# Block 0 of a one-core attention and two-expert-layer kernel: later weight splits, squares on GpSimd, single loads, two raw pieces on SP's queue

## The chip, the cores and the metric

The kernel runs on one core of one Trainium2 chip. The metric is the device time of one execution in microseconds; three executions of the kernel before are shown. One execution was also profiled, and every row below is from that one.

## What is computed

Attention with four sink tokens and a window of 128 feeds a dense layer with a squared relu, and its output feeds a layer of eight experts, of which each token uses one. The reference, cut to what matters:

```python
# q, k, v: (4, 8, 768, 64); x: 3072 tokens x 512
scores = q @ k.T / sqrt(64);  keep = is_sink | in_window        # 4 sinks, window 128
a = softmax(where(keep, scores, -1e9));  x = a @ v              # -> (3072, 512)
h = maximum(x @ w_in, 0);  x = (h * h) @ w_out                  # w_in 512 x 2048, w_out 2048 x 512
e = argmax(x @ w_gate);  g = softmax(x @ w_gate)[e];  o = sigmoid(x @ w_output_gate)[e]
out = g * o * (maximum(x @ w1[e], 0) @ w2[e])                   # 8 experts, 512 x 1024 x 512
```

The inputs `w_in` and `w_out` arrive as 64-bit floats and are turned into 32-bit ones on the chip.

## The kernel before

The 3072 tokens are 12 blocks of 256. For each block t the program makes attention (four pairs p of heads, two row groups n) and then the dense layer in 16 slices j: `l1(t, j)` multiplies by 128 columns of `w_in` and squares the relu, `l2(t, j)` multiplies by the matching rows of `w_out` and adds up in PSUM, two slices behind. The attention of block t + 1 is laid between the slices of block t. The expert layer follows after block 11, in an order written out by hand.

The order of all else is found by a planner: instructions are handed to it in the order of the program, some with a raised priority, and it fills each engine's queue by estimated times. `tc.keep_in_program_order` (also `pin`) holds instructions of one engine in the order of the program, and `behind(x, y)` places x after y without a semaphore of its own.

Weights of the dense layer come in 32 raw pieces of 512 KB (`conv(c)`; c = 2j is slice j of `w_in`, c = 2j + 1 slice j of `w_out`). The raw form has two 32-bit words for each number. Pieces 0 to 2 (`NBOOT`) have buffers of their own, `braw`, and are issued from ScalarE's queue; the others go from SP's queue into the tag "stage" with three buffers, which a few other tiles share. The inner `rest()` makes the 32-bit weights: two ScalarE activations (L327, L330) and two VectorE merges (L334, L335) into `fw[n]`, or into `fbuf` for the last eight slices of `w_out`. Block 0 multiplies by `fw` as they are ("native", L677 and L706). All other multiplications use a split into a high and a low part: `fin()` makes the high part on ScalarE (L338) and the low part on VectorE (L339). For `fbuf` it runs at once. For the native weights the program keeps it in `fins` and calls it 12 (`w_in`) or 13 (`w_out`) slices after the weights' own (`LAGS`); its subtraction waits for the native matmul that reads the weights, its ScalarE copy for nothing but the weights.

`cstep(1)` runs the next `rest()` and `fetch` issues the DMA of the next pieces but one. Ahead of block 0 a loop over half-slices h from -46 to -1 calls it at every third h, beside the attention of block 0. In block 0 it is called with each slice.

`loads(t, p, kinds)` fetches q, k and v of one pair of heads; `more(t, p)` calls it for the pair two further on. Some loads of block 0 are also called explicitly ahead of that: for pair 2, k and q are loaded by the explicit call and again by `more(0, 0)`, into the next of two buffers, and the dictionary `nat` holds the later one. `fill` issues dummy matmuls in block 0.

Of the kernel before, what the change touches and what calls it, by code (L numbers as in the profile page):

```python
# [12 lines left out]
U32 = mybir.dt.uint32  # L13
AF = mybir.ActivationFunctionType
# [26 lines left out]
NBOOT = 3  # L41
# [6 lines left out]
def kern(ctx, tc, q, k, v, n_sink, window, w_in, w_out, w_gate, w_og, w1, w2, out):  # L48
    nc = tc.nc
    V, A, G, PE, SY = nc.vector, nc.scalar, nc.gpsimd, nc.tensor, nc.sync  # L50
# [9 lines left out]
    fw = [nc.alloc_sbuf_tensor_at(f"fw{n}", [128, 512], F32, offset=w0 + 4 * (1024 * n + 512)).ap() for n in range(NF + NF // 2)]  # L60
# [226 lines left out]

    fbuf = att.tile([128, 2, 512], F32, tag="PT", name="fbuf", bufs=1)

    fins, used = {}, {}  # L290

    def after(x, y):

# [5 lines left out]
    def behind(x, y=None):  # L299

        tc.add_manual_dep(x.ins, (y or skd[0]).ins.name, mybir.DependencyInfo(mybir.DependencyClass.NoSync, mybir.DependencyReason.DATA),
                          reason="order")
        return x

    def conv(c):
        j, which = divmod(c, 2)
        if c < NBOOT:
            raw, dq = braw[c], A
        else:
            raw = cv.tile([128, 512, 2], I32, tag="stage", bufs=3, name="craw")  # L310
            dq = SY
        if which == 0:
            x = dq.dma_start(out=raw[:].rearrange("p (k f) w -> p k (f w)", k=4),
                         in_=w_in.bitcast(I32)[:, 256 * j:256 * j + 256].rearrange("(k p) f -> p k f", p=128))
            hi, lo = (WI[:, j, n].rearrange("p k f -> p (k f)") for n in range(2))
        else:
            x = dq.dma_start(out=raw[:].rearrange("p f w -> p (f w)"), in_=w_out.bitcast(I32)[128 * j:128 * j + 128, :])
            hi, lo = (WO[j // 8][:, j % 8, n] for n in range(2))
        if c < NBOOT + 2:
            tc.keep_in_program_order(x)  # L320
        if c < NBOOT:
            behind(x, brd[0])

        def rest():
            L, Hh = raw[:, :, 0], raw[:, :, 1]

            x = A.activation(out=Hh.bitcast(F32), in_=Hh.bitcast(F32), func=AF.Copy, scale=2.0 ** -112)  # L327
            if c < NBOOT:
                tc.keep_in_program_order(x)
            A.activation(out=L, in_=L.bitcast(U32), func=AF.Copy, scale=0.93 * 2.0 ** -29)  # L330
            n = NF * which + j
            f = fw[n] if n < len(fw) else fbuf[:, j % 2]
            fi = f.bitcast(I32)
            V.scalar_tensor_tensor(out=fi, in0=Hh, scalar=3, in1=L, op0=ALU.logical_shift_left, op1=ALU.bitwise_or)  # L334
            V.scalar_tensor_tensor(out=fi, in0=Hh, scalar=-2147483648, in1=fi, op0=ALU.bitwise_and, op1=ALU.bitwise_or)  # L335

            def fin():
                A.activation(out=hi, in_=f, func=AF.Copy)  # L338
                x = V.tensor_tensor(out=lo, in0=f, in1=hi.bitcast(F32), op=ALU.subtract)  # L339
                if n < len(fw):  # L340
                    after(x, used[n])

            if n < len(fw):
                fins[n] = fin
            else:
                fin()
        return rest
# [9 lines left out]
    moe.tile([128, HOME // 4], F32, name="gap1", bufs=1)  # L357
    xTs = {}

    def loads(t, p, kinds="kqvs"):  # L360
        b, u = divmod(t, NQ // 2)
        s0 = 256 * u
        for nm, src, m in (("k", k, 3), ("q", q, 2), ("v", v, 3)):
            if nm not in kinds:
                continue
            x = att.tile([128, m, 2, D], F32, tag=nm + "n", name=nm + "n", bufs=3 if nm == "v" else 2)
            lo = s0 - 128 * (m - 2)
            o = 0
            if lo < 0:
                lo, o = 0, 1  # L370
            nb = m - o
            for e in range(2):
                x_ = (A if t == 0 and (nm == "q" and p < 2 or nm == "v" and p == 0) else SY).dma_start(out=x[:, o:m, e, :],
                             in_=src[b, 2 * p + e, lo:lo + 128 * nb, :].rearrange("(n s) d -> s n d", s=128))
                if t == 0 and (p >= 2 or nm == "v"):
                    pin(x_)
                if brd and t == 0 and p < 3:
                    behind(x_, brd[0])
            nat[nm, t, p] = x
        if u == 0 and p == 0 and "s" in kinds:  # L380
            x = att.tile([H * NS, D], F32, tag="vs", name="vs", bufs=1)
            x_ = SY.dma_start(out=x[:], in_=v[b, :, 0:NS, :])
            if t == 0:
                pin(x_)
            nat["vs", b] = x
# [115 lines left out]
    def scores(t, p, n):  # L501
        i = 2 * (t % 3) + n
        W = 128 if i == 0 else 260
        c0 = KS * n if i else KS
        mask = (M0, M1, M2)[min(i, 2)]
        qt = qTt[t, p]
        kt = kTt[t, p]
        if t == 0 and n % 2:
            ps = [psX.tile([128, 512], F32, tag=f"x{e}", name=f"psx{e}") for e in range(2)]
        else:  # L510
            ps = [psS.tile([128, 512], F32, tag=f"s{e}", name=f"pss{e}") for e in range(2)]
        if t == 0:
            fill(ps[0][:, 0:W], 2)
        for e in range(2 if t < T32 else 0):
            r = slice(64 * e, 64 * e + 64)
            PE.matmul(ps[e][:, 0:W], lhsT=qt[r, 0, n, :], rhs=kt[r, 0, c0:c0 + W].bitcast(F32), start=True, stop=True)
        for e in range(2 if t >= STK else 0):
            for a_ in range(2):
                PE.matmul(ps[e][:, 0:W], lhsT=qt[:, a_, e, n, :], rhs=kt[:, e, c0:c0 + W], start=(a_ == 0), stop=(a_ == 1))
        for m, (a_, b_) in enumerate(((0, 0), (0, 1), (1, 0)) if T32 <= t < STK else ()):  # L520
            for e in range(2):
                r = slice(64 * e, 64 * e + 64)
                PE.matmul(ps[e][:, 0:W], lhsT=qt[r, a_, n, :], rhs=kt[r, b_, c0:c0 + W], start=(m == 0), stop=(m == 2))
        P = att.tile([128, 2, 260], F32, tag="P", name="P", bufs=2)
        st = att.tile([128, 8], F32, tag="st", name="st", bufs=4)
        with (tc.high_priority(100) if t >= STK else ExitStack()):
            for e in range(2):
                V.tensor_tensor_reduce(out=P[:, e, 0:W], in0=ps[e][:, 0:W], in1=mask[:, 0:W], scale=-SCALE, scalar=3.0e38,  # L528
                                       op0=ALU.add, op1=ALU.min, accum_out=st[:, e:e + 1])
        for e in range(2):  # L530
            A.activation(out=P[:, e, 0:W], in_=P[:, e, 0:W], func=AF.Exp, scale=-1.0, bias=st[:, e:e + 1],  # L531
                         accum_out=st[:, 4 + e:5 + e])
        V.tensor_scalar(out=st[:, 6:8], in0=st[:, 4:6], scalar1=1e-9, scalar2=None, op0=ALU.add)
        V.reciprocal(out=st[:, 6:8], in_=st[:, 6:8])  # L534
        if t >= T32 and i >= 2:

            V.tensor_tensor(out=P[:, :, 0:128], in0=P[:, :, 0:128], in1=P[:, :, 132:260], op=ALU.add)
            W = KS
        for e in range(2):
            if t < T32 and t + e:  # L540
                V.tensor_scalar(out=P[:, e, 0:W], in0=P[:, e, 0:W], scalar1=st[:, 6 + e:7 + e], scalar2=None, op0=ALU.mult)
            else:
                A.activation(out=P[:, e, 0:W], in_=P[:, e, 0:W], func=AF.Copy, scale=st[:, 6 + e:7 + e])  # L543
        if i >= 2:
            o = psk[n][:, 2 * p:2 * p + 2, :]
            G.tensor_copy(out=o[:, :, 0:4], in_=P[:, :, 128:132])
            G.tensor_copy(out=o[:, :, 8:12], in_=P[:, :, 128:132])
            G.tensor_tensor(out=o[:, :, 4:8], in0=P[:, :, 128:132], in1=o[:, :, 0:4].bitcast(F32), op=ALU.subtract)
        Ptile[t, p, n] = P
# [122 lines left out]
    def l1(t, j):  # L672
        ps = psH.tile([128, 256], F32, tag="h", name="psh")
        x = xTs.get(0)
# [9 lines left out]
            for n, (kk, a_, b_) in enumerate(terms):  # L684
                PE.matmul(ps[:], lhsT=WI[:, j, a_, kk, :], rhs=x[:, b_, kk, :], start=(n == 0), stop=(n == 11))  # L685
        hq = moe.tile([128, 256], F32, tag="r", name="r", bufs=2)
        A.activation(out=hq[:], in_=ps[:], func=AF.Relu)  # L687
        E_ = G if t == 0 and j % 2 else V
        if t == 0 and NF + j < len(fw):
            o = moe.tile([128, 256], F32, tag="h2", name="h32", bufs=3, padded_shape=[128, 512])  # L690
            E_.tensor_tensor(out=o[:], in0=hq[:], in1=hq[:], op=ALU.mult)
# [220 lines left out]
    braw = [boot.tile([128, 512, 2], I32, name=f"braw{n}") for n in range(NBOOT)]  # L912
# [28 lines left out]
    for h in range(-46, 0):  # L941
        run_to(h)
        if h == -42:
            masks(wide, 1)
        if h == -24:
            setup2()
        if h >= -39 and h % 3 == 0:
            cstep(1)
    bootS.close()
    wpool2 = ctx.enter_context(tc.tile_pool(name="wpool2", bufs=1))  # L950
# [4 lines left out]
    raw = None  # L955
# [113 lines left out]
    for g in range(G2):  # L1069
        t, j = divmod(g, NF)  # L1070
# [42 lines left out]
    t = NBLK - 1  # L1113
# [151 lines left out]
```

## Time and profile before

| | us |
|---|---|
| median of three executions | 1129.04 (1128.1 to 1131.95) |
| the profiled execution, its own time | 1127.99 |
| its span, first to last instruction | 1126.2 |
| first native matmul of layer 1 (L677) | 42.65 after the span's start |
| last native slice of layer 1 begins | 121.72 |
| first matmul of block 1 (L685) | 125.11 |

The profile is one execution. Engines are called PE (TensorE's matmuls), PEld (its weight loads), DVE (VectorE), ACT (ScalarE), POOL (GpSimd) and SP; a name with q (ACTq, SPq) is the engine's own queue, which issues DMAs. A row of the timeline gives start, duration, engine, line, operation, output and input tiles, and in brackets how long the engine had been idle and what ended that. Times are counted from the span's start.

### The profile page before, as it was taken

What the parts mean: (1) busy time and instruction counts of PE and PEld (TensorE: products, weight loads), DVE (VectorE), ACT (ScalarE), POOL (GpSimd) and SP (SyncE); (2) the same over time, 40 slices, a digit from 0 to 9 for tenths busy, and PEclk for the clock granted to TensorE, in tenths of its full rate; (3) what the DMA queues carried; (4) which work ended last, traced back from release to release, by engine and by line L of the source; (5) the groups of instructions that cost most, each with busy time, mean ns of one, the idle gap of its engine ahead of it and who ended that gap; (6) DMA issues with size and microseconds to landing.
All of it is one profiled execution on the core that took longest, in us unless ns stands there. A gap on an engine that the chain in (4) does not pass through costs nothing. (4 is left out here: it accounts for less than half of the span.)

```text
span 1126.2 us, 23923 instructions
## 1 busy us (share of the span) xinstructions
PE 1101.4 (98%) x6858; PEld 937.3 (83%) x6858; DVE 778.6 (69%) x2102; ACT 667.1 (59%) x1821; POOL 443.9 (39%) x989
## 2 busy tenths in 40 slices
PE   8999999999999999999999999999999999999997
PEld 4556788988999989999989999997788888888886
DVE  4789877788887778887878787567412566864144
ACT  5888877877787878787878787464222222222200
POOL 2313564346675437675336665210211222211121
PEclk9999999999999999999999999999999999999999
DMA  6677202111211111211112110395411456654111
GB/s 157 172 229 223 59 21 51 40 52 37 56 29 50 36 48 39 57 29 47 33 39 56 41 32 2 55 235 160 132 40 48 154 186 227 214 201 147 49 46 34
DMA packets 140416, 100.34 MB, mean 89 GB/s; under 512 B 104931, under 2 KB 113251, under 8 KB 140262
## 3 DMA queue, kind: packets, MB, share of 16 engines
q1 hardware_dynamic: 132020, 82.41, 26.1%
q0 software_dynamic: 5408, 14.19, 3.7%
q10 hardware_dynamic: 2834, 1.97, 0.6%
q8 instruction: 63, 1.03, 0.4%
q14 instruction: 91, 0.75, 0.3%
HBM read 85.82 MB, written 13.76 MB: 88 GB/s over the span
## 5 line engine op out<-in xcount | busy, mean ns | idle before, releaser
L685 PE MATMUL psh<-xT,WI 128*128 128x256 f32 x2112 | 283.5, 283 | 0.0
L685 PEld LDWEIGHTS psh<-xT,WI 128*128 128x128 f32 x2112 | 265.6, 188 | 7.7 <-issue 0.5
L1027 PE MATMUL psh<-WI,xt 128*128 (+1 forms) x672 | 162.1, 395 | 1.0 <-ACT xt L1007 0.7
L709 PE MATMUL psx<-WOb,h 128*128 128x512 f32 x576 | 150.0, 397 | 0.9 <-ACT h L696 0.4
L1027 PEld LDWEIGHTS psh<-WI,xt 128*128 128x128 f32 x672 | 123.8, 188 | 26.7 <-ACT xt L1007 1.4
L709 PE MATMUL psx<-WOa,h 128*128 128x512 f32 x528 | 138.7, 397 | 0.0
L694 DVE TENSOR_TENSOR r<-r 128x256 f32<-128x256 f32 x180 | 91.5, 509 | 56.8 <-ACT r L687 55.4
L1043 DVE TENSOR_TENSOR ht<-psht,ht 128x512 fp32r<-128x512 f32 x56 | 38.5, 689 | 121.1 <-ACT ht L1007 120.7
L709 PEld LDWEIGHTS psx<-WOb,h 128*128 128x128 f32 x576 | 101.9, 188 | 20.3 <-ACT h L696 2.1
L696 ACT ACTIVATE h<-r 128x256 fp32r<-128x256 f32 x184 | 76.3, 415 | 58.2 <-DVE r L694 54.3
L709 PEld LDWEIGHTS psx<-WOa,h 128*128 128x128 f32 x528 | 92.8, 188 | 15.2
L1065 POOL DMA_INDIRECT out_dram<-xg,pidx x28 | 28.4, 1016 | 189.1 <-ACT xg L1064 139.2
L697 DVE TENSOR_TENSOR h<-r,h 128x256 fp32r<-128x256 f32 x184 | 83.2, 452 | 23.5 <-ACT h L696 20.9
L576 POOL TENSOR_SCALAR_AFFINE_SELECT PT<-PT 128x256 fp32r<-128x256 f32 x224 | 98.0, 471 | 2.7 <-DVE PT L572 2.7
L531 ACT ACTIVATE P<-P,st 128x260 f32<-128x260 f32 (+1 forms) x192 | 92.5, 485 | 7.2 <-DVE st L528 3.6
L687 ACT ACTIVATE r<-psh 128x256 f32<-128x256 f32 x192 | 72.9, 380 | 34.9 <-PE psh L685 30.0
L1033 ACT ACTIVATE r<-psh 128x512 f32<-128x512 f32 x48 | 28.7, 599 | 98.5 <-PE psh L1027 96.7
L1056 PE MATMUL psy<-WOb,ht 128*128 (+1 forms) x336 | 84.0, 398 | 0.0
L612 POOL TENSOR_TENSOR xr<-tB,tC 128x128 f32<-128x128 f32 x80 | 37.9, 473 | 114.0 <-DVE tB L611 71.9
L1056 PE MATMUL psy<-WOa,ht 128*128 (+1 forms) x336 | 82.2, 392 | 0.0
L998 POOL DMA_INDIRECT xg<-x2tab,pidx x30 | 40.3, 1343 | 94.5 <-issue 51.6
L543 ACT ACTIVATE P<-P,st 128x132 f32<-128x132 f32 (+2 forms) x168 | 62.3, 415 | 20.5 <-DVE st L534 17.7
(460 smaller groups left out, 2106.6 us busy)
## 6 DMA issues: line engine op xcount, KB each, us to landing
raw<-in_moe_w_dram SPq DMA_DIRECT2D x36, 1024.0 KB
craw<-in_moe_w_out_dram SPq DMA_DIRECT2D x15, 512.0 KB
craw<-in_moe_w_in_dram SPq DMA_DIRECT2D x14, 512.0 KB
x2tab<-x2s SPq DMA_DIRECT2D x24, 256.5 KB
kn<-in_k_dram SPq DMA_DIRECT2D x64, 96.0 KB
vn<-in_v_dram SPq DMA_DIRECT2D x64, 96.0 KB
qn<-in_q_dram SPq DMA_DIRECT2D x94, 64.0 KB
kn<-in_k_dram SPq DMA_DIRECT2D x34, 64.0 KB
```

Source lines behind the costliest of these rows:

```text
L531: A.activation(out=P[:, e, 0:W], in_=P[:, e, 0:W], func=AF.Exp, scale=-1.0, bias=st[:, e:e + 1], accum_out=st[:, 4 + e:5 + e])
L543: A.activation(out=P[:, e, 0:W], in_=P[:, e, 0:W], func=AF.Copy, scale=st[:, 6 + e:7 + e])
L576: G.affine_select(out=both[:, 1 - b, e], in_=bf[:, 0, e], pattern=[[0, 2], [1 - 2 * b, 128]], compare_op=ALU.is_gt if b else ALU.is_ge, fi ...
L685: PE.matmul(ps[:], lhsT=WI[:, j, a_, kk, :], rhs=x[:, b_, kk, :], start=(n == 0), stop=(n == 11))
L687: A.activation(out=hq[:], in_=ps[:], func=AF.Relu)
L694: E_.tensor_tensor(out=hq[:], in0=hq[:], in1=hq[:], op=ALU.mult)
L696: A.activation(out=o[:, 0], in_=hq[:], func=AF.Copy)
L697: V.tensor_tensor(out=o[:, 1], in0=hq[:], in1=o[:, 0].bitcast(F32), op=ALU.subtract)
L709: PE.matmul(acc[t][m][:], lhsT=o[:, a_, 128 * m:128 * m + 128], rhs=WO[j // 8][:, j % 8, b_, :], start=(j == 0 and n == 0), stop=(j == NF ...
L998: G.indirect_dma_start(out=x, out_offset=None, in_=x2tab[:] if s >= PRE else x2tab[0:256 * (NBLK - 3)], in_offset=bass.IndirectOffsetOnAxi ...
L1027: PE.matmul(ps[:], lhsT=o[:, a_, kk, :], rhs=wview(n, par + 2048 * b_ + 512 * kk, 512), start=(c == 0), stop=(c == 11))
L1056: PE.matmul(yp[s][:], lhsT=o[:, a_, kk, :], rhs=wview(2 + n, par + 2048 * b_ + 512 * kk, 512), start=(n == 0 and kk == 0 and c == 0), stop ...
```

## The change

It has six parts. Pieces 1 and 2 are issued from SP's queue instead of ScalarE's. The two conversions of pieces 0 to 2 are placed behind the last exp that the program has issued. The ScalarE copy of a split of native weights is placed behind the last relu that the program has issued, which is that of slice 11 or 12 after the weights' own. A set `got` drops a load that was made already. All sixteen squares of block 0 are on GpSimd, where every second one was. The first `cstep` is at h = -36 instead of -39, so each piece is converted three half-slices later in the order of the program and twelve steps instead of thirteen come ahead of block 0.

```diff
-    fins, used = {}, {}
+    fins, used, exps, relu = {}, {}, [], []
...
         if c < NBOOT:
-            raw, dq = braw[c], A
+            raw, dq = braw[c], A if c == 0 else SY
...
             x = A.activation(out=Hh.bitcast(F32), in_=Hh.bitcast(F32), func=AF.Copy, scale=2.0 ** -112)
             if c < NBOOT:
-                tc.keep_in_program_order(x)
-            A.activation(out=L, in_=L.bitcast(U32), func=AF.Copy, scale=0.93 * 2.0 ** -29)
+                behind(tc.keep_in_program_order(x), exps[-1])
+            x = A.activation(out=L, in_=L.bitcast(U32), func=AF.Copy, scale=0.93 * 2.0 ** -29)
+            if c < NBOOT:
+                behind(x, exps[-1])
...
             def fin():
-                A.activation(out=hi, in_=f, func=AF.Copy)
+                x = A.activation(out=hi, in_=f, func=AF.Copy)
+                if n < len(fw):
+                    behind(x, relu[-1])
...
+    got = set()
+
     def loads(t, p, kinds="kqvs"):
...
-            if nm not in kinds:
+            if nm not in kinds or (nm, t, p) in got:
                 continue
+            got.add((nm, t, p))
...
-            A.activation(out=P[:, e, 0:W], in_=P[:, e, 0:W], func=AF.Exp, scale=-1.0, bias=st[:, e:e + 1],
-                         accum_out=st[:, 4 + e:5 + e])
+            exps.append(A.activation(out=P[:, e, 0:W], in_=P[:, e, 0:W], func=AF.Exp, scale=-1.0, bias=st[:, e:e + 1],
+                         accum_out=st[:, 4 + e:5 + e]))
...
-        A.activation(out=hq[:], in_=ps[:], func=AF.Relu)
-        E_ = G if t == 0 and j % 2 else V
+        relu.append(A.activation(out=hq[:], in_=ps[:], func=AF.Relu))
+        E_ = G if t == 0 else V
...
-        if h >= -39 and h % 3 == 0:
+        if h >= -36 and h % 3 == 0:
             cstep(1)
```

## Rows read from the trace of the kernel before

**Rows 1.** Stretches: busy us (count) per engine, granted clock, DMA share, GB/s.
```profile
12.00:18.00 6.00, 2.35 (x13) 1.26 (x13) 1.24 (x8) 4.13 (x14) 0.71 (x3) 1.00 0.84 207
18.00:24.00 6.00, 6.00 (x31) 3.13 (x29) 3.25 (x11) 2.81 (x9) 0.71 (x4) 0.72 0.43 97
42.00:125.00 83.00, 79.75 (x369) 50.42 (x369) 73.57 (x171) 71.33 (x166) 27.23 (x55) 1.00 0.68 200
100.00:165.00 65.00, 60.09 (x374) 48.65 (x375) 56.22 (x144) 50.46 (x138) 35.93 (x79) 1.00 0.29 80
125.00:165.00 40.00, 37.03 (x254) 32.29 (x253) 33.14 (x94) 28.93 (x87) 25.43 (x60) 1.00 0.11 24
165.00:1127.00 962.00, 948.10 (x6041) 834.68 (x6039) 647.02 (x1731) 539.95 (x1489) 381.60 (x819) 1.00 0.28 79
```

**Rows 2.** Timeline of TensorE up to block 0's last native slice.
```profile
12.98 0.38 PE L105 MATMUL pspt<-idle 128*128 128x512 bf16 x1 [1.08 <-ACT PT L564]
...
17.66 0.41 PE L437 MATMUL psq<-ident,qn 128*128 128x128 f32 x2 [2.67 <-DMA qn<-in_q_dram]
...
26.70 0.38 PE L397 MATMUL psk__885<-ident,kn 128*128 128x128 f32 x2
...
42.65 1.89 PE L677 MATMUL psh<-xT,fw 128*128 128x256 f32 x8
...
121.72 1.99 PE L677 MATMUL psh<-xT,fw 128*128 128x256 f32 x8
```

**Rows 3.** Timeline of ScalarE and its queue.
```profile
12.12 0.38 ACTq L313 DMA_DIRECT2D braw<-in_moe_w_in_dram  x1
12.54 0.38 ACT L564 ACTIVATE PT<-pspt 128x256 f32<-128x256 f32 x1 [1.72 <-DMA qn<-in_q_dram]
...
20.93 0.28 ACT L597 ACTIVATE xT<-psh 128x128 f32<-128x128 f32 x1 [3.91 <-PE psh L594]
...
98.70 0.36 ACT L687 ACTIVATE r<-psh 128x256 f32<-128x256 f32 x1
```

**Rows 4.** Timeline of SP's queue.
```profile
7.54 0.88 SPq L373 DMA_DIRECT2D qn<-in_q_dram  x2
...
11.91 0.88 SPq L382 DMA_DIRECT2D vs<-in_v_dram  x1
...
13.90 0.92 SPq L373 DMA_DIRECT2D qn<-in_q_dram  x2
```

**Rows 5.** Waits of TensorE and SP, 42 to 125: total us, times, longest.
```profile
PE psh L677 <- DVE fw L335: 2.3, 4, 0.9
...
SPq L317 <- DVE fw L335: 22.0, 12, 4.4
```

**Rows 6.** Timeline of VectorE: the last merge of pieces 4 and 30.
```profile
42.38 0.67 DVE L335 SCALAR_TENSOR_TENSOR fw<-craw,fw 128x512 int32<-128x512 int32 x1
...
120.99 0.68 DVE L335 SCALAR_TENSOR_TENSOR fw<-craw,fw 128x512 int32<-128x512 int32 x1
```

**Rows 7.** Stretch 44 to 100 for L338 alone, L339 alone, tile WOb alone.
```profile
44.00:100.00 56.00, 12.67 (x21) 1.00 0.72 216
...
44.00:100.00 56.00, 10.85 (x16) 1.00 0.72 216
...
44.00:100.00 56.00, 2.36 (x8) 1.43 (x8) 2.06 (x3) 2.24 (x4) 1.00 0.72 216
```

**Rows 8.** Timeline of VectorE near 143, and TensorE's waits from 125 to 165.
```profile
142.73 2.85 DVE L339 TENSOR_TENSOR WI<-fw,WI 128x512 fp32r<-128x512 f32 x3
...
PE psk__2241 L397 <- DVE PT L572: 0.7, 1, 0.7
```

**Rows 9.** Line L691, squares of slices 0 to 7: ns min/median/max, first and last start.
```profile
L691 DVE TENSOR_TENSOR h<-r x4: 414/416/419, 45.4 to 75.8; 128x256 f32<-128x256 f32 x4
L691 POOL TENSOR_TENSOR h<-r x4: 614/734/1052, 49.1 to 84.1; 128x256 f32<-128x256 f32 x4
```

**Rows 10.** Timeline of VectorE at 84.6.
```profile
84.64 1.10 DVE L335 SCALAR_TENSOR_TENSOR fw<-craw,fw 128x512 int32<-128x512 int32 x1
```

## The prediction

> **What bounds the kernel now.** I began with the busy time of the engines in stretches [rows 1]. From 165 us to the end TensorE is busy for 948 of 962 us: it is the bound there, with the same work before and after, so what this change is worth is how much sooner that stretch begins. It can only come from the time ahead of it, from the attention of block 0 up to 42 us, from the 3.25 us that TensorE idles between 42 and 125 us (the hidden layers of block 0, beside the attention of block 1), and from the 3.0 us between 125 and 165 us (the start of block 1).
>
> Then I read TensorE's timeline [rows 2]. The attention of block 0 is a chain of short steps over the engines and ends in the first matmul on native weights (L677) at 42.65. It holds two clear gaps: 1.08 us ahead of 12.98, ended by ScalarE's copy of PT, and 2.67 us ahead of 17.66, ended by the landing of a q load. After them the granted clock is 0.72 in the six microseconds from 18 to 24, where it was 1.00 before [rows 1]: the idle TensorE of 12 to 18 (2.35 of 6 us busy) was followed by a lower clock, a mix of its levels of 2.4 and 1.2 GHz, worth at most 6 x 0.28 = 1.7 us more.
>
> The two queues show why [rows 3, 4]. ScalarE's queue issues the third raw piece only at 12.12, and the PT copy behind it at 12.54 is shown as waiting for a q load: the issue stood in line for an earlier transfer, with every exp and copy of the chain behind it. On SP the q load of pair 2 is issued at 7.54 and a second time at 13.90. The transposes read the second copy, since the later call overwrites the entry in `nat`, and they start as it lands, at 17.66; the first copy was asked for six microseconds earlier.
>
> From 42 us on the waits of TensorE and of SP say one thing [rows 5]. TensorE waits for `fw` by L335, four times, 2.3 us, and SP waits 22.0 us in 12 pieces for the same line before it may issue the next raw piece. A piece goes SP, DMA, two ScalarE conversions, two VectorE merges, and frees one of three stage buffers only at the end of L335. Pieces 4 and 30 start their L335 at 42.38 and 120.99 [rows 6]: 78.6 us for 26 pieces, 3.0 each. The last native slice of layer 1 starts at 121.72, as piece 30 is done [rows 2], and the sixteen slices are (121.72 - 42.65) / 15 = 5.3 us apart, so nearly two pieces each. So the ring of conversions sets the pace of block 0, and TensorE fills nearly all of the waiting with block 1's attention. What the ring can give back is bounded by the idle 3.25 us, however much faster it gets.
>
> **No double loads, two pieces on SP.** Four issues of 64 KB leave SP (0.46 us each [rows 4]) and pair 2 of the attention uses the load of 7.54. The 2.67 us gap should go whole. Two issues (0.38 us for the later one [rows 3]) and the wait ahead of the second leave ScalarE; the 1.08 us gap should go too. Together 3.75 us, and up to 1.7 us of clock, so 5.4 at the most. At the least nothing, if the ring of conversions does not start sooner. SP now carries the pieces behind the vs load, which waited until 11.91 [rows 4]; behind them stand v of pair 2 and k, q and v of pair 3. Pair 3's k is used only at 26.70 [rows 2], over ten microseconds after its turn in SP's queue, so two issues and one more wait of 2 us are covered; without that cover such a wait costs its 2 us once. I take 3.5 us: the two gaps, little of the clock, and some of it lost to the next wait in the chain.
>
> A rule can be weighed here. The Trainium skill (DMA: Bandwidth & Descriptors, Issuing engines are not separate DMA queues) says that moving a start to another engine only saves the sequencer's time for it, usually small. By that rule the move is worth two issues of 0.38 us, and the start 2.67 + 0.76 = 3.4 us in place of 3.75. The trace shows more than the rule has: ScalarE stood idle for 1.72 us around that issue [rows 3].
>
> **Conversions later.** The twelve steps ahead of block 0 begin three half-slices later, and pieces 0 to 2 stand behind the exps of their step. Piece 4 is done at 43.05 [rows 6] for slice 2, two slices after 42.65, so some 10 us cover it; what has less cover is the ring, since piece 6 takes piece 4's buffer. If all of the early start is eaten there, the first term is nothing: a rival below.
>
> **Splits tied to the relu.** The high-part copy (L338) and the subtraction (L339) come long before block 1 reads them. In 44 to 100 us they take 12.67 us of ScalarE and 10.85 of VectorE; without those for WOb, which stay, 10.4 and 8.8 [rows 7]. Tied to the relu 11 slices after their own (slice 11's is at 98.70 now [rows 3]), all of this moves behind about 100 us. The new order is on ScalarE itself: no engine gets a wait, but VectorE's subtraction follows the copy, and block 1's slices wait for both, four slices later, which is their cover. From 42 to 125 us ScalarE loses 10.4 of 71.3 us of work and VectorE 8.8 of 73.6 [rows 1], so a piece's own chain shortens: the four waits of 2.3 us should go. Bounds: nothing, and the 3.25 us of all idle time. I take 2.3, the row that names this very wait.
>
> The work comes back in 100 to 165 us, where VectorE has 65 - 56.22 = 8.8 us idle for 8.8 us more, and ScalarE 14.5 for 10.4 [rows 1]. At the least it costs nothing, at the most 8.8 us. The nearest row: three splits in a row, 2.85 us, came ahead of a TensorE wait of 0.7 us for VectorE [rows 8]. 8.8 / 2.85 x 0.7 = 2.2 us if they came in such groups; they come one or two to a slice, so I take 1.0.
>
> **Squares on GpSimd.** Eight leave VectorE (0.416 us each, 3.3 us) for GpSimd, where the median is 0.73 [rows 9]. The product is used two slices later, some 10 us, which hides it. Against it: a merge that ran beside the last of these squares (84.1) took 1.10 us instead of the 0.67 of another [rows 6, 9, 10]; eight of those give back 8 x 0.43 = 3.4 us. I take nothing, between a gain of 3.3 and a loss of 3.4.
>
> The Trainium skill speaks against the move (SBUF — State Buffer, Who interferes with whom): a VectorE instruction with two SBUF inputs and a GpSimd one that reads SBUF block each other fully, the second waiting for the first to end. The stretched merge agrees in kind. By the rule each square could hold VectorE for its whole 0.73 us, a loss of 8 x 0.73 - 3.3 = 2.5 us of VectorE, and the sum would be -2.3 us instead of the one below.
>
> **Sum.** -3.5 - 2.3 + 1.0 + 0 = -4.8 us. The profiled execution took 1127.99 us (span 1126.2), so 1123.2 for a like one; the median of the runs shown is 1.05 us above it: 1124.2 us.
>
> **Rivals.** Changes below 0.3% (3.4 us) are what a measurement of this kernel can hardly tell from none.
> (a) The ring is no longer felt and the clock stays up: -5.4 - 3.25 = -8.7 us, 1120.4. For it speaks that two engines of the ring's chain lose an eighth of their work; against it, that of the 3.25 us only 2.3 are waits for the ring [rows 5].
> (b) The early start is eaten by the later conversions: only -2.3 + 1.0 = -1.3 us, 1127.7. For it: layer 1's last slice starts just as its piece is done. Against: ScalarE has room ahead of 42 us, 3.91 us of it in one piece up to 20.93 [rows 3].
> (c) VectorE becomes the bound from 100 to 165 us: the moved 8.8 us come on top there, the ring gains nothing, and only the start's 3.5 is kept: +5.3, 1134.3. It decides for slower where the overload costs more than the 5.8 us gained. For it: the idle time there equals the moved work. Against: conversions that run earlier leave that stretch, each with two merges of VectorE, 1.3 us, and the last splits fall behind 165 us.
> (d) The squares on GpSimd hold the merges, each beside one of the ring: -4.8 + 3.4 = -1.4, 1127.6 (by the rule of the Trainium skill above, 1126.7). One stretched merge speaks for it [rows 10]; against it, the same engine did every second square before.
> (e) The planner sorts the rest anew and nothing of the above counts: 1129.
>
> **Chances.** Forecast 0.45 (1121 to 1127 by itself), (a) 0.13, (b) 0.18, (c) 0.13, (d) 0.06, (e) 0.05. Faster by over 0.3%: 0.38 of the forecast, all of (a), little of the rest, 0.56. Slower: most of (c) and a part of (e), 0.14. Same: 0.30. The range: 1118, below (a) by most of the 3.0 us that TensorE idles after 125 us, to 1132, half way into (c).
>
> **What would show it.** No wait of TensorE for a q load near 15 us, L677 starting near 39; a granted clock near 1.00 from 18 to 24; no L338 for WI or WOa before some 95 us; the pieces from 6 on at about 2.8 us each; the last native slice near 116; VectorE above 95% from 100 to 165 us with few waits of TensorE for it. It is wrong if L677 starts early and the last native slice does not, (b), or if TensorE's idle time after 100 us grows by more than the gain, (c).

## The result and the profile after

The changed kernel took 1135.25 us (median of 6 runs, 1134.21 to 1138.61) against 1129.28 us of the kernel before beside it: a ratio of 1.0054, 95% interval 1.0038 to 1.0071. It is slower, where 1124.2 us was forecast. Its profiled execution took 1134.57 us, its span 1132.9. From the conversions' second line on the lines are numbered differently: of the names used below L335 is now L337, L338 L340, L339 L343, L397 L404, L528 L535, L572 L579, L576 L583, L602 L609, L677 L684, L685 L692, L694 L701.

First the stretches, with the columns of [rows 1].

```profile
12.00:18.00 6.00, 5.26 (x32) 2.68 (x31) 3.44 (x16) 4.93 (x17) 0.79 (x3) 1.00 0.91 244
18.00:24.00 6.00, 5.96 (x41) 3.61 (x40) 4.93 (x19) 5.86 (x17) 1.10 (x6) 1.00 0.57 127
42.00:125.00 83.00, 80.20 (x362) 50.35 (x362) 65.96 (x148) 65.40 (x152) 29.03 (x54) 1.00 0.67 200
100.00:165.00 65.00, 59.90 (x347) 46.88 (x345) 57.53 (x135) 54.31 (x144) 33.62 (x65) 1.00 0.26 69
125.00:165.00 40.00, 35.92 (x225) 29.12 (x223) 34.70 (x88) 31.45 (x89) 24.57 (x51) 1.00 0.09 21
165.00:1134.00 969.00, 952.70 (x6060) 837.64 (x6060) 652.50 (x1745) 543.77 (x1501) 384.72 (x827) 1.00 0.27 79
```

Against [rows 1], TensorE is busy 5.26 us instead of 2.35 from 12 to 18 us, and the granted clock from 18 to 24 is 1.00 instead of 0.72. From 125 to 165 us TensorE does 1.1 us less. VectorE is busy for 57.53 of 65 us from 100 to 165, hardly more than the 56.22 of before: it is not full.

Next, TensorE's timeline at the borders of the stages: the first native matmul, the last native slice, the first matmul of block 1 and that of block 2.

```profile
38.29 1.13 PE L684 MATMUL psh<-xT,fw 128*128 128x256 f32 x4 [0.70 <-SPq L642]
...
119.45 1.99 PE L684 MATMUL psh<-xT,fw 128*128 128x256 f32 x8
...
123.25 0.95 PE L692 MATMUL psh<-xT,WI 128*128 128x256 f32 x6
...
195.44 1.27 PE L692 MATMUL psh<-xT,WI 128*128 128x256 f32 x9
```

In the kernel before these starts are at 42.65, 121.72 [rows 2], 125.11 and 191.3. So the changed kernel is ahead by 4.4 us, then 2.3, then 1.9, and after block 1 it is behind by 4.1. At the end of the span it is behind by 6.7. By stage, taking each from its first matmul to the next one's:

| us | start | block 0 | block 1 | the rest |
|---|---|---|---|---|
| before | 42.65 | 82.5 | 66.2 | 934.9 |
| after | 38.29 | 85.0 | 72.2 | 937.5 |
| difference | -4.4 | +2.5 | +6.0 | +2.6 |

Block 1 in the two kernels as a stretch (the kernel before first, then the changed one), and of it the subtractions alone (L339 and L343):

```profile
125.10:191.30 66.20, 62.12 (x446) 54.71 (x443) 53.62 (x167) 47.36 (x145) 37.10 (x92) 1.00 0.14 34
...
125.10:191.30 66.20, 6.87 (x8) 1.00 0.14 34
```

```profile
123.20:195.40 72.20, 66.21 (x451) 56.19 (x450) 61.52 (x180) 55.51 (x163) 40.29 (x92) 1.00 0.13 33
...
123.20:195.40 72.20, 14.32 (x20) 1.00 0.13 33
```

Twelve more subtractions lie in block 1, 7.5 us of VectorE, nearly all of the 7.9 us by which its busy time grew. ScalarE grew by 8.2 us. So either engine could be the cause. TensorE's waits from 125 to 180 us name neither in the first place (the kernel before first, then the changed one):

```profile
PE pso L602 <- POOL PT L576: 2.0, 4, 1.0
PE psst L622 <- DVE pf L760: 1.1, 1, 1.1
PE psk__2241 L397 <- DVE PT L572: 0.7, 1, 0.7
PE psk__1991 L397 <- issue: 0.3, 1, 0.3
```

```profile
PE pso L609 <- POOL PT L583: 3.0, 5, 0.9
PE psk__2449 L404 <- DVE st L535: 1.0, 1, 1.0
PE psst L629 <- DVE pf L767: 0.7, 1, 0.7
PE psk__2235 L404 <- DVE PT L579: 0.7, 1, 0.7
PE psq L444 <- DVE st L535: 0.3, 1, 0.3
```

The waits named grew by 1.6 us, from 4.1 to 5.7, and TensorE's idle time in block 1 by 1.9, from 4.1 to 6.0. The other 4.1 of the 6.0 us stand as busy time, with 446 and 451 matmuls recorded; which delays they are made of is not shown. No wait names WI, WOa or WOb, so the split weights themselves are not seen to come late. GpSimd's selects in block 1 took no longer either (ns as min/median/max):

```profile
L576 POOL TENSOR_SCALAR_AFFINE_SELECT PT<-PT x32: 402/408/855, 127.9 to 180.2; 128x256 fp32r<-128x256 f32 x32
L583 POOL TENSOR_SCALAR_AFFINE_SELECT PT<-PT x32: 401/412/869, 128.6 to 184.3; 128x256 fp32r<-128x256 f32 x32
```

One of these stalls can be followed over three engines in the timeline: VectorE, TensorE, GpSimd.

```profile
147.77 0.69 DVE L343 TENSOR_TENSOR WOa<-fw,WOa 128x512 fp32r<-128x512 f32 x1
148.37 1.39 DVE L701 TENSOR_TENSOR r<-r 128x256 f32<-128x256 f32 x1
149.68 0.27 DVE L617 TENSOR_TENSOR tB<-pso,tB 64x128 f32<-64x128 f32 x1
...
151.36 0.42 DVE L579 TENSOR_TENSOR PT<-pspt,PT 128x256 fp32r<-128x256 f32 x1
151.69 0.68 DVE L343 TENSOR_TENSOR WI<-fw,WI 128x512 fp32r<-128x512 f32 x1
```

```profile
151.83 0.55 PE L404 MATMUL psk__2235<-ident,kn 128*128 128x128 f32 x3 [0.68 <-DVE PT L579]
...
153.85 0.87 PE L609 MATMUL pso<-PT,V 128*128 128x256 f32 x4 [0.89 <-POOL PT L583]
```

```profile
151.91 2.25 POOL L583 TENSOR_SCALAR_AFFINE_SELECT PT<-PT 128x256 fp32r<-128x256 f32 x4 [1.10 <-DVE PT L579]
```

VectorE works without a break from the split at 147.77 on. Its PT of the attention (L579) comes at 151.36, TensorE waits 0.68 us for it, and GpSimd's select, idle for 1.10 us before, starts as it is done; TensorE then waits 0.89 us for GpSimd. The wait that is put down to GpSimd begins on VectorE, one step earlier in the chain. The wait of 0.68 us is in the kernel before, too, at the same step [rows 8]; the one of 0.89 us is not. The longest wait that the kernel before does not have is that for `st`, 1.04 us, with a subtraction on VectorE shortly ahead of the step that ends it:

```profile
163.62 0.68 DVE L343 TENSOR_TENSOR WI<-fw,WI 128x512 fp32r<-128x512 f32 x1
...
165.44 0.43 DVE L535 CUSTOM_DVE_ANT_0 P<-pss,M 128x260 f32<-128x260 f32 x1
```

```profile
165.94 0.44 PE L404 MATMUL psk__2449<-ident,kn 128*128 128x128 f32 x2 [1.04 <-DVE st L535]
```

Ahead of both stalls a square (L701) is stretched as well, to 1.39 us at 148.37 and 1.23 at 162.47, where the median is 0.43. The sixteen squares of block 1 take 9.22 us instead of 7.55, so a part of VectorE's delay here is theirs. It is not needed for the loss: in `z_sub_tied` below they take 8.09 us, and block 1 is longer still.

### The profile page after: what moved, and what is told of

Same layout as the page of the kernel before. It is cut to its first block, busy times and chain, and to the rows that moved or that the text cites. A ratio compares the mean times of both kernels' runs of the same rounds, so it can differ in the third digit from the quotient of the medians.

```text
span 1132.9 us, 23918 instructions
## 1 busy us (share of the span) xinstructions
PE 1106.0 (98%) x6858; PEld 938.4 (83%) x6858; DVE 779.9 (69%) x2094; ACT 667.6 (59%) x1821; POOL 450.6 (40%) x997
## 5 line engine op out<-in xcount | busy, mean ns | idle before, releaser
L692 PE MATMUL psh<-xT,WI 128*128 128x256 f32 x2112 | 285.5, 283 | 0.0
L692 PEld LDWEIGHTS psh<-xT,WI 128*128 128x128 f32 x2112 | 266.3, 188 | 8.9 <-issue 0.5
L701 DVE TENSOR_TENSOR r<-r 128x256 f32<-128x256 f32 x176 | 91.8, 522 | 54.3 <-ACT r L694 52.8
L583 POOL TENSOR_SCALAR_AFFINE_SELECT PT<-PT 128x256 fp32r<-128x256 f32 x224 | 98.3, 473 | 6.5 <-DVE PT L579 6.4
L694 ACT ACTIVATE r<-psh 128x256 f32<-128x256 f32 x192 | 72.9, 380 | 32.9 <-PE psh L692 27.6
L535 DVE CUSTOM_DVE_ANT_0 P<-pss,M 128x260 f32<-128x260 f32 (+1 forms) x184 | 68.0, 398 | 15.8 <-PE pss L523 7.8
L1005 POOL DMA_INDIRECT xg<-x2tab,pidx x30 | 41.0, 1366 | 91.7 <-issue 52.5
```

The lines of the kernel that those rows point to most:

```text
L583: G.affine_select(out=both[:, 1 - b, e], in_=bf[:, 0, e], pattern=[[0, 2], [1 - 2 * b, 128]], compare_op=ALU.is_gt if b else ALU.is_ge, fi ...
L694: relu.append(A.activation(out=hq[:], in_=ps[:], func=AF.Relu))
L701: E_.tensor_tensor(out=hq[:], in0=hq[:], in1=hq[:], op=ALU.mult)
L1005: G.indirect_dma_start(out=x, out_offset=None, in_=x2tab[:] if s >= PRE else x2tab[0:256 * (NBLK - 3)], in_offset=bass.IndirectOffsetOnAxi ...
```

## The experiments

The ratios are to the kernel before on the same chip, with 95% intervals. The experiments ran on four chips: the four from `x1_no_tie` to `x4_old_squares` on one, those with y and z on another, `r_before`, `r_no_tie`, `x7_got` and `x8_sp` on a third, `r_after` and `x6_notie_oldsq` on a fourth. The kernel before took 1131.3 to 1133.7 us on them, so a time that was expected from the first result's 1129 us is to be read by its ratio. Stages are held against both profiles of the kernel before, the one above and `r_before`.

**Nothing changed, and the changed kernel again.** `r_before` is the kernel before, `r_after` the changed one.

> The kernel before, unchanged, profiled and timed as if it were a change, on the chip of the next three. Every theory expects a ratio of 1.000; how far its interval lies from that is what such a comparison can tell. Its stages are the ones to hold the next three against: if this chip is slower outside blocks 0 and 1 too, block 1 should still take 66 to 67 us.

> The changed kernel, unchanged. Theory (the subtractions in block 1 cost it some 6 us, and the rest of the change gives back some 2): ratio 1.002 to 1.006 as on the first chip, block 1 at 72 us, first native matmul near 38.3 us. Rival (the first result was that chip's): 0.998 to 1.001.

Measured: 1.0001 (0.9984 to 1.0018) and 1.0077 (1.0053 to 1.0101). Block 1 took 66.1 and 72.7 us, with 8 and 20 subtractions in it, as on the first chip. The loss is the change's; the second ratio lies above the range that was expected for it. The start differs: the kernel before began block 0 only at 46.4 us in its second profile, the changed one at 38.6.

**The tie taken out, and the tie alone.**

```diff
-                x = A.activation(out=hi, in_=f, func=AF.Copy)
-                if n < len(fw):
-                    behind(x, relu[-1])
+                A.activation(out=hi, in_=f, func=AF.Copy)
```

The tie is the line `behind(x, relu[-1])`. `x1_no_tie`, run again as `r_no_tie`, is the changed kernel with this edit; `x2_tie_alone` is the kernel before with the opposite one.

> The changed kernel with the splits free again (no order behind the relu), all else as changed. Theory (late splits overload VectorE, ScalarE and the port that GpSimd shares in block 1): block 1, which took 66.2 us before and 72.2 us after the change, comes back to 66 to 67 us, the start at 38.3 us stays, and the whole is 1125 to 1129 us. Rival (the squares on GpSimd, the later conversions or a new order of everything cost it): block 1 stays above 70 us and the whole at 1134 to 1136 us.

> The changed kernel without the tie, once more, in more rounds and beside a profile of the kernel before from the same chip. Theory (without the tie the rest of the change is a small gain): ratio 0.996 to 0.999; the first native matmul 3.5 to 4.5 us sooner than in the kernel before on this chip, block 1 within 1 us of it, so that what is missing of the 4 us was given back in block 0, by the ring of conversions. Rival (the first result was chance): 0.999 to 1.002.

> The kernel before with the tie of the splits to the relu alone. Theory of the late splits: the start stays at 42.6 us, block 0 runs a little faster (first matmul of block 1 at 122 to 125 us), block 1 takes 71 to 73 us instead of 66.2, the whole is 1133 to 1137 us. Rival (another part of the change costs it): block 1 stays at 66 us, the whole at 1126 to 1130 us.

Measured: 0.9977 (0.9963 to 0.9991) and 0.9980 (0.9967 to 0.9993) without the tie, 1.0051 (1.0032 to 1.0070) with the tie alone. The tie costs the whole loss; the other five parts together are a gain of 0.2% in two runs, small but beyond their intervals, and that version beats both kernels. Block 1 took 66.4 and 66.5 us without it, 72.1 with it.

**Which half of the split.** `z_copy_tied` and `z_sub_tied` are the kernel before with one half late.

```diff
# z_copy_tied
+                if n < len(fw):
+                    x = V.tensor_tensor(out=lo, in0=f, in1=f, op=ALU.subtract)
+                    behind(A.activation(out=hi, in_=lo.bitcast(F32), func=AF.Copy), relu[-1])
...
# z_sub_tied
                 x = V.tensor_tensor(out=lo, in0=f, in1=hi.bitcast(F32), op=ALU.subtract)
                 if n < len(fw):
+                    behind(x, sqs[-1])      # sqs: the squares that run on VectorE
```

> The kernel before, in which ScalarE's high-part copies of the 24 native slices wait for the relu 12 or 13 slices on, while VectorE's subtraction stays as early as before (here it runs ahead of the copy and takes f from f, so the low parts are zero and only the time counts). Theory: it is VectorE's late subtractions that lengthen block 1, where VectorE also has the attention's softmax; then block 1 (first hidden matmul of block 1 to that of block 2) stays at 66 to 67 us, and the ratio to before lies at 0.998 to 1.001. Rival: it is ScalarE's copies, put ahead of the exps and relus of block 1, that cost; then block 1 takes about 72 us and the ratio is about 1.005. If each costs a part, 69 us.

> The kernel before, in which only VectorE's 24 subtractions are late (tied to the last square on VectorE, at the place of the relu tie); ScalarE's copies stay where the planner puts them. Theory (VectorE's late subtractions): block 1 about 72 us, ratio about 1.005. Rival (ScalarE's copies): block 1 66 to 67 us, ratio 0.998 to 1.001. If each costs a part, 69 us.

Block 1 as a stretch (columns of [rows 1]), in `z_copy_tied`, `z_sub_tied`, `r_no_tie` and `r_before`:

```profile
124.80:192.10 67.30, 64.75 (x449) 55.48 (x449) 52.71 (x169) 55.70 (x164) 37.35 (x92) 1.00 0.14 35
```

```profile
125.10:198.60 73.50, 68.80 (x452) 58.82 (x450) 61.07 (x180) 47.30 (x145) 42.21 (x92) 0.95 0.13 32
...
135.00:155.00 20.00, 17.93 (x88) 14.49 (x87) 14.97 (x38) 10.47 (x32) 11.47 (x24) 0.83 0.09 21
```

```profile
124.10:190.60 66.50, 63.52 (x452) 55.45 (x449) 51.70 (x166) 47.95 (x147) 36.47 (x93) 1.00 0.14 36
```

```profile
129.30:195.40 66.10, 61.90 (x446) 54.63 (x443) 53.17 (x166) 47.07 (x145) 37.01 (x92) 1.00 0.14 34
```

With the copies late, ScalarE has its 55.70 us in block 1 and block 1 takes 67.3 us: ScalarE's 8 us more cost at most about one. With the subtractions late and ScalarE as before, it takes 73.5 us and the ratio is 1.0044 (1.0026 to 1.0063). Two engines got the same additional work, and only VectorE's lengthens block 1. In `z_sub_tied` the granted clock falls to 0.83 for 20 us, worth 20 x 0.17 = 3.4 us, so there a part of the loss is the clock's. In `r_after` and `x2_tie_alone` it is 0.83 for 10 us of block 1 (144 to 154 and 149 to 159 us), 1.7 us each. The changed kernel's first profile lost 6.0 us at a clock of 1.00, so the clock is not needed for it. The total of `z_copy_tied` (1221.28 us, 1.0802) is not to be compared, and its expectation was wrong in that: the copy reads the zero low part, so both parts of these weights are zero, and the expert layer runs on other values, with 720 matmuls of its first layer instead of 672. That the times in block 1 don't hang on the values was not tried.

**A shorter tie.** `y_tie4` is the changed kernel with the `fin` called 4 or 5 slices after the weights' own.

> The changed kernel with the lag of 4 and 5 slices in place of 12 and 13, so that most tied splits fall between the sixth slice of block 0 and its end, where VectorE and ScalarE have idle time. Theory (what counts is how much split work lies inside block 1): block 1 at 66 to 68 us and a ratio of 0.997 to 1.000. Rival (the tie itself, any place of it, spoils the planner's order): block 1 about 72 us and 1.005.

Measured: 1.0016 (0.9998 to 1.0034). Six subtractions are left in block 1, and it takes 67.4 us: not the tie but what it puts into block 1 costs there. The total is outside the expected range. In its profile block 0 took 88.2 us, with 13 subtractions between 100 us and its end where the changed kernel has 8 (and the kernel before 8); that these cost the rest was not tried.

All profiles, by the subtractions that lie in block 1:

| kernel | subtractions in block 1 | VectorE busy, us | granted clock | block 1, us |
|---|---|---|---|---|
| `x1_no_tie`, `r_no_tie` | 4, 4 | 51.6, 51.7 | 1.00, 1.00 | 66.4, 66.5 |
| `z_notie_oldh` (below) | 4 | 50.8 | 1.00 | 64.6 |
| `y_tie4` | 6 | 53.2 | 1.00 | 67.4 |
| `x3_loads_sp` (below) | 6 | 51.8 | 1.00 | 66.1 |
| `x7_got` (below) | 7 | 52.5 | 1.00 | 66.4 |
| `z_copy_tied` | 8 | 52.7 | 1.00 | 67.3 |
| before, `r_before` | 8, 8 | 53.6, 53.2 | 1.00, 1.00 | 66.2, 66.1 |
| `x6_notie_oldsq` (below) | 9 | 53.8 | 1.00 | 66.9 |
| `x8_sp` (below) | 9 | 54.8 | 1.00 | 67.6 |
| `x4_old_squares` (below) | 19 | 61.3 | 1.00 | 71.5 |
| `x2_tie_alone` | 19 | 62.1 | 0.98 | 72.1 |
| after, `r_after` | 20, 20 | 61.5, 61.6 | 1.00, 0.98 | 72.2, 72.7 |
| `z_sub_tied` | 20 | 61.1 | 0.95 | 73.5 |

With 4 to 9 of them block 1 takes 64.6 to 67.6 us, and the kernel before lies within that; 11 or 12 more than it has cost 5.3 to 7.4 us, of which some 4 to 6 are left where the lower clock is taken off. The clock fell in block 1 in three of the five profiles with 19 or 20, and in none of the other eleven.

**The start, part by part.** `x7_got` is the kernel before with single loads only, `x8_sp` with the two pieces on SP only, `x3_loads_sp` with both; `z_notie_oldh` is the changed kernel without the tie and with the conversion steps as before (h from -39).

> The kernel before with the second loads of pair 2 left out and nothing else. The prediction put 2.67 us of the start on this part. Theory (the gap ahead of the transposes of pair 2 is the second load's and goes with it): the first native matmul 2 to 3 us sooner than in the kernel before on this chip; block 0 then takes as much longer, since the pieces come no faster, and the ratio is 0.998 to 1.000. Rival (the gap moves to the next transfer): the first native matmul within 1 us of before, ratio 1.000.

> The kernel before with the second and third raw piece on SP's queue and nothing else. The prediction put 1.08 us of the start on this part. Theory: the first native matmul about 1 us sooner, ratio 0.999 to 1.000. Rival (on SP the two pieces stand ahead of loads of pairs 2 and 3, which come later): the first native matmul later than before, ratio 1.000 to 1.002.

> The kernel before with single loads and with two raw pieces on SP's queue, nothing else. Theory: the two gaps of 1.1 and 2.7 us go and the first native matmul starts at 38 to 40 us instead of 42.65; about half of it is still there at the first matmul of block 1 and the whole is 1125 to 1128 us. Rival (the ring of conversions takes all of it back): first matmul of block 1 at 125 us and the whole at 1129 us.

> The changed kernel without the tie and with the conversion steps from h = -39 on, as before. The changed kernel without the tie starts its hidden layers 4.4 us sooner than before but has a block 0 of 88.0 us against 82.4, so that the start is given back. Theory A (the later conversion steps delay the ring of pieces): block 0 comes down to about 85 us and the ratio from 0.9977 to about 0.995. Theory B (the ring is paced by its own DMA and buffers, at 3.0 us a piece, whatever the steps ahead of it): the ring's end stays within 1 us of the changed kernel without the tie, and the ratio stays at 0.997 to 0.999.

Measured: 1.0007 (0.9995 to 1.0020), 0.9992 (0.9977 to 1.0007), 0.9983 (0.9966 to 1.0001), 1.0002 (0.9987 to 1.0018). None of the four is faster than before by more than its interval, and the last fits neither range that was expected for it. TensorE's longest waits from 8 to 30 us in `x7_got`, `x8_sp` and `x3_loads_sp`, one fence each:

```profile
PE psq L440 <- DMA qn<-in_q_dram: 5.2, 2, 2.8
```

```profile
PE pss L516 <- ACT qT L446: 3.6, 1, 3.6
```

```profile
PE pss L519 <- ACT qT L449: 2.4, 1, 2.4
```

And stretches between 12 and 24 us, two of `r_before` and one each of `x7_got`, `z_notie_oldh` and `r_no_tie`:

```profile
12.00:18.00 6.00, 2.88 (x14) 1.41 (x13) 0.74 (x5) 2.02 (x8) 1.28 (x6) 0.85 0.57 159
18.00:24.00 6.00, 4.62 (x20) 2.55 (x19) 2.41 (x11) 2.37 (x8) 0.45 (x3) 0.50 0.59 123
```

```profile
18.00:24.00 6.00, 3.58 (x14) 1.64 (x14) 1.06 (x7) 1.99 (x6) 0.00 (x0) 0.50 0.46 104
```

```profile
12.00:18.00 6.00, 4.42 (x21) 2.49 (x22) 2.35 (x10) 4.47 (x15) 2.17 (x13) 0.81 0.87 240
```

```profile
12.00:18.00 6.00, 5.34 (x33) 2.87 (x31) 3.49 (x15) 4.81 (x15) 1.11 (x4) 1.00 0.82 231
```

Taken alone, single loads leave the wait for q and the SP queue leaves one for the copy of qT: in either a gap stays, and the first native matmul comes at 45.7 and 45.1 us against 46.4 in `r_before`. Both together leave 2.4 us of gap (39.9 us). With the later conversions as well that gap is gone and the clock stays at 1.00 (38.9 us in `r_no_tie`), in six profiles of seven; in the seventh, `y_tie4`, two waits of 0.8 and 0.7 us were left, the clock was 0.73 from 12 to 18 us, and the start came at 40.0. For the ring the comparison is inconclusive: `z_notie_oldh` reaches block 1 at 127.5 us, the same kernel with the later steps at 126.8 in one profile (`x1_no_tie`) and at 124.1 in another (`r_no_tie`). In the first two the granted clock was 0.79 for 8 us (98 to 106 and 105 to 113), worth 1.7 us each; in the third it was 1.00. Whether the place of the conversion steps matters for the ring stays open; the whole time with the earlier steps is 0.002 higher, with intervals that overlap.

**The squares.** `x4_old_squares` is the changed kernel, `x6_notie_oldsq` the one without the tie, both with every second square of block 0 on VectorE as before.

```diff
-        E_ = G if t == 0 else V
+        E_ = G if t == 0 and j % 2 else V
```

> The changed kernel with every second square of block 0 back on VectorE. Theory of the late splits: no difference beyond 1.5 us from the changed kernel, 1134 to 1137 us, block 1 above 70 us. Rival (squares on GpSimd hold the merges of the ring): the last native slice starts 2 to 4 us sooner than the 119.4 us of the changed kernel and the whole is 1131 to 1133 us.

> The changed kernel without the tie and with every second square of block 0 on VectorE, as before. Theory (the squares move VectorE's work where it has room, and the merges of the ring come no sooner or later): the ratio stays at 0.997 to 1.000, within 0.002 of the changed kernel without the tie. Rival (the squares on GpSimd hold VectorE's merges): block 0 shorter by 2 us or more and a ratio of 0.994 to 0.996. Other rival (the squares on VectorE delay the ring): block 0 longer by 2 us or more and a ratio of 1.000 to 1.003.

Measured: 1.0075 (1.0049 to 1.0102) and 1.0009 (0.9991 to 1.0027). With the tie that is `r_after`'s 1.0077, though above the 1.0054 of the first result; without it, the old squares are 0.003 above the new ones, at the edge of the two intervals and a little more than expected. So the squares on GpSimd show no loss, and may be worth a little.

## Why the prediction was wrong

**The failed step is the term of +1.0 us for the splits moved into 100 to 165 us.** What it said of the work was right: the first copy for WI is at 101.95 us, and all of it went behind that. Its price was 6.0 us. The step took VectorE's 8.8 idle us in that stretch as room for 8.8 us of work, and priced one group of splits by one wait of 0.7 us [rows 8], which is still there after the change. But VectorE's idle time there lies between the steps of a chain over four engines (scores, exp, transposes, PT, select, output), and the splits went to where they were in front of such steps, as at 147.77 above. VectorE never came near the 95% at which the prediction looked for trouble: it is busy for 88% of 100 to 165 us and 85% of block 1, and the chain is late all the same. The bound that the prediction had written down, at most 8.8 us, held for block 1.

By size the ring's term, below, failed almost as far: block 0 took 2.5 us more where -2.3 stood. With the start's -4.4, block 1's +6.0 and +2.6 from block 2 on this makes the +6.7 us of span. The term of the splits decides the sign, for without the tie the ratio is 0.998.

That is rival (c) by its place and its sign. That its time came close (1134.3 forecast, 1135.25 measured) is luck: it has +8.8 us for the splits and nothing for block 0 and for the time from block 2 on. Its mechanism, an engine that becomes the bound, is not what the trace shows: the engine is delayed, not full. Its chance of 0.13 leaned on the argument that earlier conversions leave the stretch. They left no room, since the ring did not end much earlier.

**The start, -3.5 us: about right in size (-4.4 measured), wrong in its parts.** The gaps of 1.08 and 2.67 us are gone and the clock from 18 to 24 us is 1.00. But the 2.67 us were not the second load's alone: without it, TensorE waits for q all the same (`x7_got`). Both parts together bring it to 39.9 us (`x3_loads_sp`). The later conversions, which the prediction had down as a cost at most, are in all six profiles that began at 38.3 to 39.1, but also in `y_tie4`, at 40.0.

**The ring of conversions, -2.3 us: wrong.** The last merge of piece 6 before, and of pieces 6 and 30 in the changed kernel:

```profile
52.77 0.69 DVE L335 SCALAR_TENSOR_TENSOR fw<-craw,fw 128x512 int32<-128x512 int32 x1
```

```profile
50.18 1.03 DVE L337 SCALAR_TENSOR_TENSOR fw<-craw,fw 128x512 int32<-128x512 int32 x1
...
118.71 0.68 DVE L337 SCALAR_TENSOR_TENSOR fw<-craw,fw 128x512 int32<-128x512 int32 x1
```

And ScalarE's waits for raw pieces from 40 to 125 us, before and after:

```profile
ACT craw L327 <- DMA craw<-in_moe_w_in_dram: 2.5, 4, 1.0
ACT craw L327 <- DMA craw<-in_moe_w_out_dram: 1.4, 3, 0.7
```

```profile
ACT craw L327 <- DMA craw<-in_moe_w_in_dram: 6.7, 6, 1.7
...
ACT craw L327 <- DMA craw<-in_moe_w_out_dram: 2.8, 4, 1.5
```

In the kernel before, piece 30 is merged at 120.99 [rows 6]: from piece 6 to piece 30 that is 2.84 us a piece before and 2.86 after. The pieces were to come every 2.8 us, and they did so already before; the prediction's 3.0 counted from piece 4 and so took in the longer step from piece 5 to 6 (44.78 to 52.77). ScalarE and VectorE lost the work that was counted (65.40 and 65.96 us busy instead of 71.33 and 73.57), but ScalarE then stood waiting for raw pieces to land, 9.5 us instead of 3.9. The failed step is that a piece's own chain would shorten. Worked out from the starts of the issues, the conversions (L327) and the last merges of pieces 6 to 30, a piece took in the mean 4.85 us before and 4.79 after from its issue to its first conversion, and 3.51 and 3.40 us from there to the end of its last merge. The splits taken away had hardly stood in its way. TensorE's waits for L337 fell from 2.3 us [rows 5] to 1.5.

Of the early start 2.1 us were given back before the last native slice, nearly all of it early: the fourth slice, which reads piece 6, begins at 52.50 instead of 54.63, a lead of 2.1 us where the first had 4.4. That is what rival (b) foretold, but its reason is not shown: `x3_loads_sp`, with the conversions where they were, started at 39.9 us and had its fourth slice only at 54.9.

**The squares, 0: right.** In sum the merges beside them did not stretch more than before. Line L337 before 119 us, ns as min/median/max:

```profile
L337 DVE SCALAR_TENSOR_TENSOR fw<-craw,fw x19: 677/693/1096, 47.7 to 118.7; 128x512 int32<-128x512 int32 x19
```

In the kernel before the same line had 672/689/1104. Of all 21 merges into `fw`, 4 took over 0.72 us there, three of them 1.10 (one is [rows 10]), and 7 in the changed kernel, from 0.75 to 1.10; together they took 15.9 and 16.0 us. The rule that spoke against the move, in the Trainium skill (SBUF — State Buffer, Who interferes with whom), shows elsewhere in this trace: the square of 1.39 us at 148.37 above ran beside a GpSimd instruction on x2U and x2T (L753, 148.00 to 149.49), and the one of 1.23 us at 162.47 beside another (162.24 to 163.41). For the merges in sum the move changed nothing.

**What the sum did not have.** The prediction took the time from 165 us on for the same before and after. But 2.6 us are lost after block 2 begins: 0.9 in block 9 (58.9 and 59.8 us) and 1.4 from the first slice of block 11 on. `r_no_tie` takes 940.3 us from block 2's start to the end and `r_before` 937.9: 2.4 us are lost without the tie too. ScalarE's timeline in the changed kernel shows one place:

```profile
749.57 1.92 ACT L984 ACTIVATE WOa<-raw 128x2048 fp32r<-128x2048 f32 x1 [1.65 <-DMA raw<-in_moe_w_dram]
...
751.48 0.89 ACT L694 ACTIVATE r<-psh 128x256 f32<-128x256 f32 x2
```

A copy of expert weights, 1.92 us, has waited for its DMA ahead of two relus of the last block. In the kernel before the same line (L977) waited 0.9 us instead of 1.65. Whether the time was lost by this order, and why the change brings it, was not tried.

## What to carry to other kernels

Idle time of an engine need not be room for more work. Where the engine is one link of a chain over several engines, its idle time lies between the steps of that chain, and work that is put in front of a step can delay the rest: here 7.5 us of subtractions came with 6.0 us, at 85% busy. Before work is moved into a stage, look at which chain passes through its engine there: ScalarE's 8 us in the same stage cost at most about one. And work taken off an engine shortens a ring only where a piece had to wait behind that work, so follow one piece through all its parts first.

## What the runs showed of the chip

The same program began block 0 at 42.65 us in one profile and at 46.4 us in another. In both TensorE stood idle for over half of 12 to 18 us. After it the granted clock was 0.72 from 18 to 24 us in the one, worth 6 x 0.28 = 1.7 us, and 0.85, 0.50 and 0.79 in the three stretches of 6 us from 12 to 30 in the other, worth 6 x 0.86 = 5.2 us. Six profiles without such a gap (after, `r_after`, `x1_no_tie`, `r_no_tie`, `x4_old_squares`, `x6_notie_oldsq`) stayed at 1.00 over all of 12 to 42 us and began at 38.3 to 39.1 us; in `y_tie4` two short waits, 1.5 us together, went with a clock of 0.73 from 12 to 18. A gap early on cost its own length and a share of the lower clock that varied from profile to profile.
